# Score units one piece earlier in two steps, one query tile transposed by DMA, one bound from sums of squares

## The chip, the cores and the metric

The kernel runs on one core of a Trainium2 chip. The metric is the device time of one execution in microseconds (us); the median of several is quoted. The record calls an execution slow when it is over 1.5% above the fastest of its kernel, and fast otherwise; ratios use the fast ones.

In the profiles PE is TensorE (matmuls), PEld its weight loads, DVE VectorE, ACT ScalarE, POOL GpSimd; SPq is the queue of SyncE, which here issues the stores and the transposes by DMA. L435 is line 435 of the kernel; the change shifts the lines, so the same instruction is L439 after it.

## The reference, cut to what matters

```python
scores = scale * np.matmul(q, k.transpose(0, 1, 3, 2))      # 8 batches, 8 heads, 576 tokens, head_dim 64
...
scores = np.where(causal, -1000000000.0, scores + np.minimum(bias, 0.0))
scores = scores - np.max(scores, axis=-1, keepdims=True)
attn = np.exp(scores)
attn = attn / (np.sum(attn, axis=-1, keepdims=True) + 1e-09)
x = np.matmul(attn, v)        # then as x: 4608 tokens x 512
...
h = x @ w_in                  # 512 -> 2048, layer 1
g = 0.5 * h * (1.0 + erf(h * inv_sqrt2))
out = g @ w_out               # 2048 -> 512, layer 2
```

The output is 4608 x 512 in fp32.

## The kernel before: the parts that matter

The MLP (layers 1 and 2) runs over nine chunks of 512 tokens. While chunk c is in it, the attention of batch b = c + 1 is threaded through chunk c's layer 2. This layer 2 has four sub-tiles of 128 tokens, 16 matmuls each, in 16 pieces of 4 matmuls; after each piece come the side items listed for it.

```python
def groups(c, subs, side):
    n = len(side)
    for i in range(n):
        l2_item(c, subs, i * FT // n, (i + 1) * FT // n)   # matmuls; at the end of a sub-tile copy and store
        for f, *a in side[i]:
            f(*a)

# chunks 1 to 6 (b = c + 1)
sc_at = (2, 5, 7, 9) if b < 4 else (2, 5, 8, 11)           # score units: 16 or 24 matmuls, then two exps on ACT
...
for at, (g, u) in zip((5, 8, 10 if b < 4 else 11, 12 if b < 4 else 14), ...):
    side[at].append((mk, b, g, u))                         # causal mask, DVE
for at, (g, it) in zip((6, 7, 9, 10), [(0, 0), (0, 1), (1, 0), (1, 1)]):
    side[at].append((av, b, g, it))                        # P @ V on PE, reciprocal and x on DVE
if b < 4:
    side[12].append((av, b, 0, 2))
    side[13].append((av, b, 1, 2, True))                   # True: no transpose by DMA
    side[14].append((to_xT, b, 2, True))                   # four PE transposes and a DVE copy
if c == 1:
    side[0].extend([(absmax, c, 0), (absmax, c, 1)])
    side[3].append((cert_exp,))
```

An x tile must be transposed into xT before layer 1 reads it: by PE, or by a DMA from SP's queue:

```python
def to_xT(b, it, pe=False):
    ...
    if not pe:
        nc.sync.dma_start_transpose(out=xT[:, :, t0 : t0 + n], in_=x[:n, :])
        return
    ...
```

A certificate at the end checks that bounds on q, k and v hold, among them the largest |q| and |k|. It takes them from absmax (a reduction on DVE) or, for batch 0, from sums of squares (ACT, accumulated). Otherwise a slow general path runs; it never does on this data.

## Time and profile before

| | before |
|---|---|
| median, first three executions | 315.59 us |
| span of the profiled run, granted clock | 314.2 us, 0.999 |
| PE / DVE / ACT busy | 96% / 63% / 61% |
| layer 2 of chunk 1 | 70.77 to 89.02 us: 18.24 us |
| layer 2 of chunk 2 | 103.80 to 121.88 us: 18.08 us |

The lengths of phases are the differences between the starts of the first matmul of each layer in the timeline (o_ps is layer 2, h_ps layer 1), taken before rounding. The two phases, as the answer on windows gives them for the kernel before; columns are length, then busy time and number of instructions of PE, weight load, DVE, ACT, POOL, the clock, the share of DMA and GB/s:

```profile
70.77:89.02 18.25, 17.90 (x187) 8.97 (x189) 15.04 (x25) 11.90 (x12) 2.60 (x4) 1.00 0.76 171
...
103.80:121.88 18.08, 17.82 (x186) 9.14 (x188) 12.74 (x36) 11.34 (x11) 2.60 (x4) 1.00 0.79 174
```

PE is full in both, DVE is not; yet step 1 is 0.16 us longer than step 2, and the list of waits has one entry that says why:

```profile
PEld L435 <- DVE P L367: 0.6, 1, 0.6
```

One P @ V product (P is the matrix of exps of the scores, masked) had its weight load held up for 0.6 us by a mask on DVE; it is the first product of step 1, at 78.42 us.

### The profile page before, as it was taken

What the parts mean: (1) busy time and instruction counts of PE and PEld (TensorE: products, weight loads), DVE (VectorE), ACT (ScalarE), POOL (GpSimd) and SP (SyncE); (2) the same over time, 40 slices, a digit from 0 to 9 for tenths busy, and PEclk for the clock granted to TensorE, in tenths of its full rate; (3) what the DMA queues carried; (4) which work ended last, traced back from release to release, by engine and by line L of the source; (5) the groups of instructions that cost most, each with busy time, mean ns of one, the idle gap of its engine ahead of it and who ended that gap; (6) DMA issues with size and microseconds to landing.
All of it is one profiled execution on the core that took longest, in us unless ns stands there. A gap on an engine that the chain in (4) does not pass through costs nothing. (4 is left out here: it accounts for less than half of the span.)

```text
span 314.2 us, 6059 instructions
## 1 busy us (share of the span) xinstructions
PE 302.0 (96%) x2475; PEld 155.5 (49%) x2516; DVE 199.0 (63%) x398; ACT 191.0 (61%) x258; POOL 54.5 (17%) x73
## 2 busy tenths in 40 slices
PE   8899999999999999999999999999999999999993
PEld 3477755544554455545454455444544555444441
DVE  7776658599769856975598459955895532250020
ACT  2786878887737673875586658756776666105400
POOL 8653341133001500070007000500000000000000
PEclk9999999999999999999999999999999999999999
DMA  7999999779521973179307951633101331010012
GB/s 124 222 230 209 225 211 270 163 140 211 141 84 25 199 173 102 22 166 206 102 17 171 190 118 36 143 79 91 50 19 42 102 52 26 33 72 32 1 68 75
DMA packets 30979, 36.46 MB, mean 116 GB/s; under 512 B 15648, under 2 KB 20000, under 8 KB 30944
## 3 DMA queue, kind: packets, MB, share of 16 engines
q0 software_dynamic: 11552, 23.07, 38.1%
q1 hardware_dynamic: 19248, 12.80, 14.4%
q8 instruction: 21, 0.34, 0.4%
q14 instruction: 14, 0.11, 0.1%
q10 hardware_dynamic: 144, 0.13, 0.1%
HBM read 36.85 MB, written 9.44 MB: 147 GB/s over the span
## 5 line engine op out<-in xcount | busy, mean ns | idle before, releaser
L483 PE MATMUL o_ps<-w_out_r,gT 128*128 128x512 bf16 x551 | 132.2, 379 | 2.4 <-issue 1.6
L467 PE MATMUL h_ps<-xT,w_in_r 128*128 128x512 bf16 (+1 forms) x625 | 131.4, 357 | 1.3 <-DVE xT L413 0.5
L472 ACT ACTIVATE gT<-h_ps 128x1024 bf16<-128x1024 f32 (+1 forms) x80 | 75.1, 939 | 64.5 <-PE h_ps L467 63.7
L467 PEld LDWEIGHTS <-w_in_r 128*128 128x128 bf16 x640 | 59.8, 98 | 54.2 <-issue 0.6
L483 PEld LDWEIGHTS <-gT 128*128 128x128 bf16 x576 | 51.9, 98 | 56.6 <-issue 3.0
L359 ACT ACTIVATE P<-sc_ps 128x1024 bf16<-128x1024 f32 x56 | 54.3, 1021 | 30.5 <-PE sc_ps L344 30.5
L122 POOL DMA_DIRECT2D raw_v<-in_v_dram x40 | 34.1, 863 | 128.4 <-ACT sq L213 115.7
L493 DVE COPY o_sb<-o_ps 128x512 f32<-128x512 f32 x31 | 21.4, 691 | 46.5 <-PE o_ps L483 46.5
L444 DVE RECIPROCAL rc<-av 128x4 f32<-128x4 f32 (+1 forms) x80 | 14.0, 175 | 39.4 <-PE av L435 39.3
L187 DVE STREAM_TRANSPOSE qkT<-raw_qk 128x576 f32<-128x576 f32 x32 | 37.4, 1242 | 1.8 <-DMA raw_qk<-in_k_dram 1.7
L445 DVE TENSOR_TENSOR x<-av,rc 128x256 bf16<-128x256 f32 (+1 forms) x80 | 33.8, 423 | 3.0
L435 PEld LDWEIGHTS <-P 128*128 128x128 bf16 x576 | 27.1, 97 | 16.5 <-issue 0.8
L205 DVE TENSOR_REDUCE amx<-raw_qk 128x2 f32<-128x2304 bf16 x14 | 35.1, 2532 | 0.0
L435 PE MATMUL av<-vv,P 128*128 128x65 bf16 x576 | 30.5, 193 | 0.6 <-POOL vv L221 0.2
L367 DVE TENSOR_TENSOR P<-P,tri_bf 128x1024 bf16<-128x1024 bf16 (+1 forms) x33 | 22.0, 669 | 9.1 <-ACT P L359 9.1
L221 DVE TENSOR_TENSOR vv<-raw_v,wb 128x512 bf16<-128x512 f32 (+1 forms) x39 | 25.4, 690 | 2.5 <-DMA raw_v<-in_v_dram 2.5
L213 ACT ACTIVATE sq<-raw_v 128x512 bf16<-128x512 f32 (+1 forms) x40 | 24.8, 621 | 0.0
L344 PE MATMUL sc_ps<-qkT 32*128 32x256 bf16 (+2 forms) x560 | 18.2, 250 | 0.0
L344 PEld LDWEIGHTS <-qkT 32*128 32x128 bf16 x560 | 11.7, 92 | 12.4 <-issue 11.6
L498 ACT ACT_TABLE_LOAD x8 | 10.3, 1283 | 0.9 <-PEq L817 0.8
L419 PE MATMUL f_ps<-zero 128*128 128x512 bf16 x26 | 9.3, 494 | 1.2 <-DVE zero L150 1.2
L501 ACT ACT_TABLE_LOAD x8 | 10.3, 1283 | 0.1
(81 smaller groups left out, 92.3 us busy)
## 6 DMA issues: line engine op xcount, KB each, us to landing
out_dram<-o_sb SPq DMA_DIRECT2D x35, 256.0 KB, 2.2
raw_v<-in_v_dram POOLq DMA_DIRECT2D x32, 256.0 KB, 5.5
raw_qk<-in_q_dram POOLq DMA_DIRECT2D x7, 576.0 KB, 7.5
raw_qk<-in_k_dram POOLq DMA_DIRECT2D x7, 576.0 KB, 10.4
w_in_r<-in_moe_w_in_dram POOLq DMA_DIRECT2D x4, 512.0 KB, 12.1
w_out_r<-in_moe_w_out_dram POOLq DMA_DIRECT2D x4, 512.0 KB, 15.8
raw_v<-in_v_dram POOLq DMA_DIRECT2D x8, 128.0 KB, 6.4
raw_qk<-in_q_dram POOLq DMA_DIRECT2D x2, 288.0 KB, 6.2
```

Of the source, the lines that this page charges most:

```text
L122: eng.dma_start(out=t[:n_st, st, :, :], in_=bass.AP(tensor=v.tensor, offset=v.offset + b * H * S * D + st * 128 * D, ap=[[D, n_st], [S * D ...
L187: nc.vector.transpose(qkT[b % 2][:, i, g, :S, :].rearrange("p s e -> p (s e)").bitcast(fp32) .rearrange("p (l j) -> p j l", j=LT), raws[b, ...
L205: nc.vector.tensor_reduce(amx[:, b * HG + g], raws[b, "qk"][:, :, g, :], axis=AX, op=ALU.max, apply_absolute_value=True,)
L213: nc.scalar.activation(sq[:n_st], raws[b, "v"][:n_st, st].rearrange("p h d -> p (h d)"), func=AF.Square, accum_out=sumv[:n_st, b, st : st ...
L221: eng.tensor_tensor(vv[b % 2][:n_st, st, :, 0:D], raws[b, "v"][:n_st, st, :, :], w.unsqueeze(2).to_broadcast([n_st, H, D]), op=MULT,)
L344: nc.tensor.matmul(s_ps[h // 2][:, h % 2, off : off + n], lhsT=qk[r, 1, g, jt * 128 : jt * 128 + 128, e], rhs=qk[r, 0, g, i0 : i0 + n, e], ...
L359: nc.scalar.activation(P[:, 2 * h2 : 2 * h2 + 2, o : o + 512], s_ps[h2], func=AF.Exp, scale=scale)
L435: nc.tensor.matmul(o_ps[:, h, :], lhsT=P[:, h, off : off + 128], rhs=vv[b % 2][:, jt, 4 * g + h, :], start=(i == 0), stop=(i == len(BLK[it ...
L445: nc.vector.tensor_tensor(x_of[b, it][:n, g * 256 : g * 256 + 256].rearrange("p (h d) -> p h d", d=D), o_ps[:n, :, 0:D], rc[:n].unsqueeze( ...
L467: nc.tensor.matmul(h_ps[:, i, :], lhsT=w_in_r[:, ko, ft * 128 : (ft + 1) * 128], rhs=xT[:, ko, c * NB + n0 : c * NB + n1], start=(ko == 0) ...
L472: nc.scalar.activation(gT_of[c][:, f2 * 2 : f2 * 2 + 2, n0:n1], h_ps, func=AF.Gelu)
L483: nc.tensor.matmul(y_of[c, sub], lhsT=gT[:, ft, sub * 128 : (sub + 1) * 128], rhs=w_out_r[:, ft, :], start=(ft == 0), stop=(ft == FT - 1),)
```

## The change

It has three parts, for steps 1 and 2 (chunks 1 and 2). The score units, the first mask and the products of query tiles 0 and 1 move up one piece of layer 2; the other three masks and the products of tile 2 move up two. Query tile 2 is transposed by DMA and no longer by PE. And the bound for batch 1's group 1 is taken by two squares on ACT, so that DVE has one absmax (2.5 us) less ahead of step 1's masks.

```diff
-                sc_at = (2, 5, 7, 9) if b < 4 else (2, 5, 8, 11)
+                sc_at = (1, 4, 6, 8) if b < 4 else (2, 5, 8, 11)
...
+                mk_at = (4, 6, 8, 10) if b < 4 else (5, 8, 11, 14)
...
+                av_at = (5, 6, 8, 9) if b < 4 else (6, 7, 9, 10)
...
                 if b < 4:
-                    side[12].append((av, b, 0, 2))
-                    side[13].append((av, b, 1, 2, True))
-                    side[14].append((to_xT, b, 2, True))
+                    side[10].append((av, b, 0, 2))
+                    side[11].append((av, b, 1, 2))
                 if c == 1:
-                    side[0].extend([(absmax, c, 0), (absmax, c, 1)])
+                    side[0].append((absmax, c, 0))
+                    side[12].extend([(square_qk, c, 1, 0), (square_qk, c, 1, 1)])
```

(Cut: `square_qk` gets the batch as an argument, and the certificate adds 0.25 to three pairs of sums in three small instructions.)

More of the change, by code (lines that the diff above doesn't have):

```diff
@@ L191, in tr_qk, with square_qk @@
         )
-    ssq = const.tile([128, HG, 2], fp32, name="ssq")
-    def square_qk(g, i):
-        r = raws[0, "qk"][:, i, g, :]
+    ssq = const.tile([128, 2 * HG, 2], fp32, name="ssq")
+    BY_SQ = [(0, 0), (0, 1), (1, 1)]
+    def square_qk(b, g, i):
+        r = raws[b, "qk"][:, i, g, :]
         nc.scalar.activation(
             r, r, func=AF.Square, scale=D ** -0.5,
-            accum_out=ssq[:, g, i : i + 1],
+            accum_out=ssq[:, b * HG + g, i : i + 1],
         )
@@ L288, in cert_1 @@
         cg[0] = g = const.tile([128, 3], fp32, name="cg")
-        nc.vector.tensor_scalar(amx[:, 0:HG, :], ssq, 0.25, None, op0=ALU.add)
+        for bb, gg in BY_SQ:
+            j = bb * HG + gg
+            nc.vector.tensor_scalar(amx[:, j], ssq[:, j], 0.25, None, op0=ALU.add)
         for i in range(2):
@@ L628 @@
                 side[9] = [(av, b, 0, 3)]
-                side[11] = [(av, b, 1, 2, True), (scale_v, b, 4), (square_qk, 0, 0), (square_qk, 0, 1)]
-                side[12] = [(av, b, 1, 3, True), (square_qk, 1, 0), (square_qk, 1, 1)]
+                side[11] = [(av, b, 1, 2, True), (scale_v, b, 4), (square_qk, 0, 0, 0), (square_qk, 0, 0, 1)]
+                side[12] = [(av, b, 1, 3, True), (square_qk, 0, 1, 0), (square_qk, 0, 1, 1)]
                 side[13] = [(to_xT, b, 2, True)]
@@ L642 @@
                 side[sc_at[3]].append((gelu_set,))
-                for at, (g, u) in zip((5, 8, 10 if b < 4 else 11, 12 if b < 4 else 14), [(0, 0), (1, 0), (0, 1), (1, 1)]):
+                mk_at = (4, 6, 8, 10) if b < 4 else (5, 8, 11, 14)
+                for at, (g, u) in zip(mk_at, [(0, 0), (1, 0), (0, 1), (1, 1)]):
                     side[at].append((mk, b, g, u))
-                for at, (g, it) in zip((6, 7, 9, 10), [(0, 0), (0, 1), (1, 0), (1, 1)]):
+                av_at = (5, 6, 8, 9) if b < 4 else (6, 7, 9, 10)
+                for at, (g, it) in zip(av_at, [(0, 0), (0, 1), (1, 0), (1, 1)]):
                     side[at].append((av, b, g, it))
                 if b < 4:
-                    side[12].append((av, b, 0, 2))
-                    side[13].append((av, b, 1, 2, True))
-                    side[14].append((to_xT, b, 2, True))
+                    side[10].append((av, b, 0, 2))
+                    side[11].append((av, b, 1, 2))
                 if c == 1:
-                    side[0].extend([(absmax, c, 0), (absmax, c, 1)])
+                    side[0].append((absmax, c, 0))
+                    side[12].extend([(square_qk, c, 1, 0), (square_qk, c, 1, 1)])
                     side[3].append((cert_exp,))
```

## The prediction

> **What bounds the kernel now.** I read the page first (engine shares, then the groups), then the timeline of all engines through layer 2 of chunk 2, then the answer on the tile xT, then the waits. The page, with PE's clock row and the groups that the change touches:
>
> ```profile
> PE 302.0 (96%) x2475; PEld 155.5 (49%) x2516; DVE 199.0 (63%) x398; ACT 191.0 (61%) x258; POOL 54.5 (17%) x73
> ...
> PEclk9999999999999999999999999999999999999999
> ...
> L205 DVE TENSOR_REDUCE amx<-raw_qk 128x2 f32<-128x2304 bf16 x14 | 35.1, 2532 | 0.0
> ...
> xT<-x SPq DMA_TRANSPOSE x29, 2.4
> ```
>
> PE is busy 96% of a 314.2 us span at full clock; DVE and ACT have slack on average. So the time is the length of PE's instruction stream plus its few gaps. Time saved on DVE or ACT counts only where PE waits for it. The change touches the layer-2 phases of chunks 1 and 2 only (steps 1 and 2; batches 2 and 3 are then in attention). The end of step 2 before, from the timeline of all engines:
>
> ```profile
> 115.04 0.64 PE L344 MATMUL sc_ps<-qkT 32*128 32x256 bf16 x24
> 115.61 0.30 PE L435 MATMUL av<-vv,P 128*128 128x65 bf16 x4
> 115.72 1.94 ACT L359 ACTIVATE P<-sc_ps 128x1024 bf16<-128x1024 f32 x2 [0.72 <-PE sc_ps L344]
> ...
> 117.31 0.17 DVE L444 RECIPROCAL rc<-av 128x4 f32<-128x4 f32 x1
> 117.52 0.42 DVE L445 TENSOR_TENSOR x<-av,rc 128x256 bf16<-128x256 f32 x1
> 117.67 1.28 ACT L501 ACT_TABLE_LOAD   x1
> 117.92 0.69 DVE L493 COPY o_sb<-o_ps 128x512 f32<-128x512 f32 x1
> ...
> 118.53 0.68 DVE L367 TENSOR_TENSOR P<-P,tri_bf 128x1024 bf16<-128x1024 bf16 x1
> ...
> 119.33 0.18 DVE L444 RECIPROCAL rc<-av 128x4 f32<-128x4 f32 x1
> ...
> 120.80 0.39 PE L410 MATMUL xt_ps<-ident_bf,x 128*128 128x128 bf16 x4
> ...
> 121.88 0.59 PE L467 MATMUL h_ps<-xT,w_in_r 128*128 128x512 bf16 x2
> ```
>
> Columns are start, duration, engine, line, operation. PE goes from the last score unit (115.04) through the PE transposes (120.80) to the next chunk's layer 1 (121.88) with no hole over 0.1 us. In step 1 the same marks are 82.16, 87.93 and 89.02. The transposes by DMA, from the answer on xT:
>
> ```profile
> L406 SPq DMA_TRANSPOSE xT<-x x29: 1171/1196/1992, 62.0 to 264.1; - x29
> ...
> DMA to landing us min/median/max: 2.3/2.4/7.0
> ```
>
> A DMA transpose takes SP's queue 1.2 us and lands 2.4 us after issue as a median, worse when the loads are running.
>
> **What the Trainium skill says.** (1) "TensorE: Matmul & The Clock Gate", Part 4: PE-mode transpose: the result goes to PSUM and needs a DVE copy after; about 390 ns alone, 275 ns in one kernel. Here the four transposes of a tile are pipelined: PE's next matmul starts 0.22 us after the first of them (120.80 to 121.02), and the copy is the 0.42 us row at 121.22. (2) "VectorE: DVE Perf Modes", The three transpose paths: 1309 ns for a 128x128 block by DMA; the trace has 2.4 us for four blocks with their completion, and that is what I use. (3) The same page, The perf-mode tier table: tensor_reduce runs at 1x only. The trace agrees: 2532 ns for 2304 elements, the costliest single DVE instruction. (4) "DMA: Bandwidth & Descriptors", Issuing engines are not separate DMA queues: all DMAs share the same 16 engines. The trace agrees: the two transposes issued at 181.2 and 182.5 us, when loads still run (the table of windows gives a DMA share of 1.09 at 178 to 180 and 0.73 at 180 to 182 us), land after 4.1 and 3.2 us instead of 2.4.
>
> **The change, part by part.**
> Which token tiles matter: layer 1 of chunk c reads tokens 512c to 512c+511. For chunk 2 that includes batch 2 (from token 1152) up to its token 384, so query tiles 0 to 2; for chunk 3 it is batch 3's tiles 0, 1 and half of 2. Tile 2 must therefore be in xT before the first matmul of the next layer 1. That is why it was transposed on PE, close to its use.
>
> (a) PE transposes removed: four in each of two steps, 0.22 us of PE stream each step, on the path: -0.44 us. The copy (0.42 us of DVE) also goes; it is off the path.
>
> (b) All score units, masks and attention-times-V products go up one piece of layer 2 (4 matmuls; eight take 116.86 to 118.58, so 0.86 us a piece). Nothing is added on PE, order and spacing remain. The first unit now comes 8 matmuls after the start of layer 2, 72.5 us in step 1; it needs the PSUM tile of the last gelu, free at 71.99. No new wait.
>
> (c) One absmax (2.5 us) leaves DVE in step 1. Before, the four ran 67.25 to 77.16, so the first mask came at 77.69 to 78.36 and PE's first product at 78.42: the waits list 0.6 us of PEld behind that mask in one case. The distance from second score unit to end of the fourth is 76.72 to 82.75 = 6.03 us in step 1 against 109.75 to 115.61 = 5.86 us in step 2, where DVE is not late. So it is worth 0.17 us.
>
> (d) Two ACT squares with their accumulator reads, about 1.15 us each by the four that exist (52.78 to 57.37 is 4.59). They come after the gelu table load ending at 86.1; ACT then sat idle 4.92 us before the gelu at 91.00. Hidden. The two extra small DVE operations in the certificate, in the last chunk, are some 0.3 us by neighbours of 0.14 to 0.2, off the path.
>
> (e) Added: a DMA transpose of tile 2 whose landing PE must await. The chain from the end of the last score unit, with before's own durations: to the exp's start 0.11 (115.61 to 115.72), two exps 1.94, hand-over 0.03, mask pair 0.80 (118.53 to 119.33), reciprocal and x of group 0 0.61 (117.31 to 117.92), the store's copy 0.61 (117.92 to 118.53; the instruction order puts it between the two x), reciprocal and x of group 1 0.63, SP's start 0.06, landing 2.45, PE's restart 0.05 (estimate, from other hand-overs). Sum 7.29 us. PE's own work in the same stretch: before 121.88 - 115.61 = 6.27, less 0.22 transposes, plus one piece 0.86 = 6.91. **So PE arrives 0.38 us early and waits.**
>
> The end of the step: the last score unit ends at 115.61 - 0.86 = 114.75 in step 2, and at 82.75 - 0.86 - 0.17 = 81.72 in step 1. Adding 7.29: layer 1 starts at 122.04 (before 121.88: +0.16) and 89.01 (before 89.02: -0.01). **Sum +0.15 us.** I add 0.05 for the 256 KB store of the third sub-tile, which SP issues just ahead of the transpose on the same rings: 315.59 + 0.2 = 315.8.
>
> **The rivals.**
> 1. The transpose is hidden. Then the gain is what PE loses: 0.22 in step 2, 0.39 in step 1, so 315.0. For it: DMA is quiet there (the share of DMA is 0.09 at 116 to 118 us). Against it: the chain above, short by 0.38 us in both steps.
> 2. The transpose lands late, as under load (3.2 to 4.1 us): PE waits 0.8 to 1.7 us more in each step, 317 to 319. For it: the store just ahead in the queue. Against it: that store's own landing is 2.2 us after issue, in both steps, and the big loads of step 2 end near 116 us, of step 1 near 82 us.
> 3. DVE was a hidden bound in step 1, so that freeing 2.5 us shortens it by more. Against: DVE idles 1.31 us before the reciprocal at 83.09, so it has caught up by then; I count 0.17.
> 4. ACT becomes late for the next gelu: needs over 4.9 us of new work, there is 2.7 at most.
>
> **Range and chances.** The sum is +0.2; rival 1 gives -0.6, a partly late landing +1. I give the main chain about 60%, rival 1 25%, rival 2 10%. Runs of before lie within 0.4 us. The range is 315.0 to 316.6. 2% is 6.3 us, which no rival reaches: within 2% at 0.97, faster 0.01, slower 0.02.
>
> **What would show each step.** In the changed profile: L410 group down from 44 to 36 transposes and 31 DMA transposes instead of 29; 13 absmax, 6 squares of raw_qk; the first mask of step 1 no longer holding up PE; a wait of PE (or PEld) at L1's first matmul (layer 1) for a DMA xT of 0.3 to 0.5 us, twice, which does not exist before; layer 1 of chunks 2 and 3 starting within 0.3 us of 89.0 and 121.9. The prediction is wrong if that wait is absent, or is over 1 us because the landing of these two transposes is over 3 us, or if later phases, which I take as a mere shift, change length.

## The result and the profile after

The changed kernel took 315.64 us (median of 6 runs, 314.98 to 316.12), the kernel before 315.7 us in the same rounds (6 runs, 314.78 to 316.66). The ratio is 0.9994, 95% interval 0.997 to 1.0017: the same. The ratio is made from the fast runs of the same rounds, so not quite the ratio of the medians.

From the page of the changed kernel, the lines of PE and of the absmax group:

```profile
PE 305.0 (97%) x2508; PEld 155.0 (49%) x2508; DVE 196.2 (62%) x397; ACT 193.4 (62%) x262; POOL 54.5 (17%) x73
...
L207 DVE TENSOR_REDUCE amx<-raw_qk 128x2 f32<-128x2304 bf16 x13 | 32.6, 2535 | 0.0
```

One absmax is gone (2.5 us less on DVE). PE's busy time seems to rise by 3 us, but that is records and not work: the trace of before lacks 25 of the 576 layer-2 matmuls and 15 of the 640 of layer 1, this one lacks none. For the same reason no conclusion is drawn from PE's counts of these two groups. The counts that the prediction named came out: 36 PE transposes (44 before), 31 DMA transposes (29), 13 absmax, 6 squares; and the list of waits no longer has a product held up by a mask.

The end of step 2 in the changed kernel, from the timeline of all engines, the counterpart of the lines in the prediction:

```profile
114.01 0.64 PE L348 MATMUL sc_ps<-qkT 32*128 32x256 bf16 x24
...
114.58 0.30 PE L439 MATMUL av<-vv,P 128*128 128x65 bf16 x4
...
114.69 1.94 ACT L363 ACTIVATE P<-sc_ps 128x1024 bf16<-128x1024 f32 x2 [0.72 <-PE sc_ps L348]
...
116.66 0.69 DVE L371 TENSOR_TENSOR P<-P,tri_bf 128x1024 bf16<-128x1024 bf16 x1
...
117.47 0.17 DVE L448 RECIPROCAL rc<-av 128x4 f32<-128x4 f32 x1
...
118.02 0.68 DVE L497 COPY o_sb<-o_ps 128x512 f32<-128x512 f32 x1
118.03 3.62 PE L487 MATMUL o_ps<-w_out_r,gT 128*128 128x512 bf16 x16
...
118.73 0.34 SPq L499 DMA_DIRECT2D out_dram<-o_sb  x1
118.82 0.42 DVE L449 TENSOR_TENSOR x<-av,rc 128x256 bf16<-128x256 f32 x1
119.28 1.20 SPq L410 DMA_TRANSPOSE xT<-x  x1
...
121.82 1.89 PE L471 MATMUL h_ps<-xT,w_in_r 128*128 128x512 bf16 x8 [0.17 <-issue]
```

PE now does its last four pieces in one run, the 16 matmuls from 118.03. Matmuls of this size start every 0.216 us, so the next could start at 121.49. It starts at 121.82: a hole of 0.33 us, of which the row shows 0.17 (the end of the row before is modelled). The label "issue" says that the profile found no releaser. The transpose was issued at 119.28; its landing, asked for that instruction alone:

```profile
L410 SPq DMA_TRANSPOSE xT<-x x1: 1195/1195/1195, 119.3 to 119.3; - x1
...
DMA to landing us min/median/max: 2.5/2.5/2.5
```

Taken before rounding, the transposes of tile 2 landed at 88.76 and 121.73 us, and layer 1 began 0.09 us after them in both steps. So the time fits the DMA, but the profile doesn't name it; this needed experiments.

Phase by phase, from these two traces:

| phase | before | changed |
|---|---|---|
| layer 1 of chunk 1 | 14.30 | 14.30 |
| layer 2 of chunk 1 (step 1) | 18.24 | 18.18 |
| layer 1 of chunk 2 | 14.78 | 14.78 |
| layer 2 of chunk 2 (step 2) | 18.08 | 18.20 |
| each phase of chunks 3 to 7 and layer 1 of chunk 8 | the same in both | within 0.01 |
| from layer 2 of chunk 8 to the end | 19.18 | 19.32 |

Before rounding, step 1 is 0.06 us shorter and step 2 is 0.11 us longer. All else is a shift, except the very end. That end and the stretch ahead of chunk 1 differ between any two runs: in the ten traces the former is 18.50 to 19.90 us, and the start of chunk 1's layer 2 lies between 69.68 and 71.60 us. They differ between runs of the same kernel too (70.67 and 71.60 us in the two traces of the changed kernel), so they count here as noise of the total time.

### The profile page after: what moved, and what is told of

It reads as the page before. It is cut to its first block, busy times and chain, and to the rows that moved or that the text cites. A ratio compares the mean times of both kernels' runs of the same rounds, so it can differ in the third digit from the quotient of the medians.

```text
span 314.3 us, 6094 instructions
## 1 busy us (share of the span) xinstructions
PE 305.0 (97%) x2508; PEld 155.0 (49%) x2508; DVE 196.2 (62%) x397; ACT 193.4 (62%) x262; POOL 54.5 (17%) x73
## 5 line engine op out<-in xcount | busy, mean ns | idle before, releaser
L487 PE MATMUL o_ps<-w_out_r,gT 128*128 128x512 bf16 x576 | 135.6, 379 | 0.0
L207 DVE TENSOR_REDUCE amx<-raw_qk 128x2 f32<-128x2304 bf16 x13 | 32.6, 2535 | 0.0
```

Source lines behind the costliest of these rows:

```text
L207: nc.vector.tensor_reduce(amx[:, b * HG + g], raws[b, "qk"][:, :, g, :], axis=AX, op=ALU.max, apply_absolute_value=True,)
L487: nc.tensor.matmul(y_of[c, sub], lhsT=gT[:, ft, sub * 128 : (sub + 1) * 128], rhs=w_out_r[:, ft, :], start=(ft == 0), stop=(ft == FT - 1),)
```

## The experiments

The theory: taking the transposes off PE and the mask wait out of step 1 saves about 0.6 us, but PE then waits 0.33 us for the DMA transpose of tile 2, in both steps, and that gives it back. The rival: the hole ahead of layer 1 is a start-up cost that the profile calls issue and has nothing to do with the DMA. Eight runs were made, of six new kernels and two repeats, all correct. The phases of the two steps:

| run | step 1 | step 2 | ratio to before of its rounds |
|---|---|---|---|
| before | 18.24 | 18.08 | |
| changed | 18.18 | 18.20 | 0.9994 (0.997 to 1.0017) |
| changed, again (e7) | 18.16 | 18.18 | 0.9984 (0.997 to 0.9997) |
| e1: tile 2 on PE again | 18.09 | 18.09 | one run |
| e2: store emitted later | 17.86 | 17.86 | 0.9988 (0.995 to 1.0025) |
| e8: e2 again | 17.86 | 17.86 | 0.9957 (0.9943 to 0.9971) |
| e3: an extra DMA transpose | 19.58 | 19.54 | 1.007 (1.0043 to 1.0097) |
| e4: before, tile 2 by DMA only | 19.68 | 19.52 | 1.0074 (1.0051 to 1.0096) |
| e5: absmax back on DVE | 19.18 | 18.16 | 1.0007 (0.9988 to 1.0026) |
| e6: before, squares only | 18.09 | 18.09 | one run |

**e1, the transposes of tile 2 on PE again.**

```diff
-                    side[11].append((av, b, 1, 2))
+                    side[11].append((av, b, 1, 2, True))
+                    side[14].append((to_xT, b, 2, True))
```

> The changed kernel, but query tile 2 is transposed on PE again (four transposes and the DVE copy, three pieces after its last product); everything else of the change stays. Theory (the new transpose by DMA lands 0.33 us after PE has run dry, and this wait eats what the change saves): the hole ahead of layer 1 in chunks 2 and 3 is gone, 0.22 us of transposes are back, so both layer-2 phases take 18.08 us instead of 18.18 and 18.20; span 0.2 us shorter than the changed kernel. Rival (the hole is a start-up cost of layer 1 that the profile calls issue, and has nothing to do with the DMA): the hole stays at 0.16 us or more and both phases take 18.4 us.

Measured: 18.09 us in both. With the transposes back on PE the steps are 0.1 us shorter than with the DMA. So in the place where it stands, the DMA transpose costs more PE time (0.33 us of hole) than the 0.22 us it removes. The single run of 315.0 us proves nothing by itself; the phases do. They are also those of e6 below (18.09), which moves nothing: moving the units up by itself saves no time, it only makes room for the DMA.

**e2, the store of the third sub-tile after the last product of tile 2.**

```diff
         for i in range(n):
-            l2_item(c, subs, i * FT // n, (i + 1) * FT // n)
+            l2_item(c, subs, i * FT // n, (i + 1) * FT // n, store=not (c in (1, 2) and subs == (2,)))
...
                     side[11].append((av, b, 1, 2))
+                    side[11].append((l2_store, c, (2,)))   # the copy and store of l2_item, as a function
```

> The changed kernel, but in chunks 1 and 2 the copy and store of the third sub-tile are emitted after the last product of query tile 2, so that the reciprocal and x of group 1 no longer stand behind the 0.61 us copy on DVE, nor the transpose behind the store on the queue. Theory: the transpose is issued 0.6 us earlier, lands 6.7 us after the end of the last score unit, PE needs 6.9 us, so PE no longer waits: both phases take 17.86 us (0.33 us less than the changed kernel's), span 0.66 us shorter than the changed kernel, time ratio against before about 0.998. Rival (start-up cost): phases unchanged at 18.2 us, no gain.

Measured: 17.86 us in both phases, as the theory said. The end of step 1 in e2, from PE's own timeline:

```profile
84.09 3.62 PE L487 MATMUL o_ps<-w_out_r,gT 128*128 128x512 bf16 x16
87.55 1.89 PE L471 MATMUL h_ps<-xT,w_in_r 128*128 128x512 bf16 x8
```

From the first of the 16 matmuls to layer 1 it is 3.46 us, which is 16 times 0.216; in the changed kernel it was 3.78 and 3.79 us (85.07 to 88.85, 118.03 to 121.82). The hole is gone, and nothing was done to layer 1. A start-up cost would have stayed: the rival is out. The transpose of tile 2 in step 1:

```profile
L410 SPq DMA_TRANSPOSE xT<-x x1: 1190/1190/1190, 85.0 to 85.0; - x1
...
DMA to landing us min/median/max: 2.5/2.5/2.5
```

Before rounding it landed at 87.42, 0.13 us ahead of layer 1 at 87.55 (0.15 in step 2). In the runs in which PE waits, layer 1 began 0.09 us after the landing, so the spare is about 0.04 to 0.06 us (an estimate from these numbers). One size was not as expected: counted from the product after the last score unit, the transpose was issued 4.32 us later (80.64 to 84.96), in the changed kernel 4.69 (81.62 to 86.31). That is 0.37 us earlier and not 0.6, since DVE, freed of the copy, now waits for PE's last products of tile 2 (83.85 to 84.26) before its reciprocal at 84.29. It was just enough.

**e3, one more DMA transpose ahead of tile 2's.**

```diff
+                    side[11].append((to_xT, b, 1))         # repeats tile 1, the same values
                     side[11].append((av, b, 1, 2))
```

> The changed kernel with one more DMA transpose on the same queue, a repeat of query tile 1 just ahead of that of tile 2, in steps 1 and 2; the result stays right. Theory: tile 2's transpose starts about 1.3 us later, PE waits that much longer, phases of 19.5 us each, 2.6 us in all. Rival (PE doesn't wait for this transpose): no change.

Measured: 19.58 and 19.54 us. The two transposes of step 1 on the queue, and the end of step 1 from PE's timeline:

```profile
85.89 2.50 SPq L410 DMA_TRANSPOSE xT<-x  x2
...
84.53 3.62 PE L487 MATMUL o_ps<-w_out_r,gT 128*128 128x512 bf16 x16
89.70 1.89 PE L471 MATMUL h_ps<-xT,w_in_r 128*128 128x512 bf16 x8 [1.56 <-issue]
```

The delay passes one for one to PE, again under the label "issue": 5.17 us between the two starts where 3.46 are matmuls. In this trace that label ahead of layer 1 is the wait for a landing. e2 moved the store along with the copy; e3 leaves both where they were, so it is the transpose that PE waits for and not the store. The kept traces say it more sharply: in the two steps of all five runs in which PE waits (changed, e7, e3, e4, e5) layer 1 began 0.09 us after the landing of tile 2's transpose, ten times of ten, whether the wait was 0.3 or 1.7 us. One run (granted clock 0.979) took 323.32 us.

**e4, tile 2 by DMA without moving the units.**

```diff
-                    side[13].append((av, b, 1, 2, True))
-                    side[14].append((to_xT, b, 2, True))
+                    side[13].append((av, b, 1, 2))
```

(This is an edit of the kernel before.)

> The kernel before with one thing changed: query tile 2 of batches 2 and 3 is transposed by DMA; no unit is moved, absmax stays. Theory: x of tile 2 is done 5.16 us after the end of the last score unit, the transpose lands 2.5 us later, so layer 1 starts 7.7 us after it instead of 6.27: each phase 1.43 us longer (19.67 and 19.51 us), 2.9 us in all, time ratio against before 1.009. Rival (taking transposes off PE is what counts): 0.44 us shorter.

Measured: 19.68 and 19.52 us, within 0.01 us of what the chain gave. The transposes by DMA alone make the kernel 0.7% slower; moving the units and tile 2's products up is what pays for their latency.

**e5, the absmax back on DVE, in the changed kernel.**

```diff
-                    side[0].append((absmax, c, 0))
-                    side[12].extend([(square_qk, c, 1, 0), (square_qk, c, 1, 1)])
+                    side[0].extend([(absmax, c, 0), (absmax, c, 1)])
```

(And the certificate's list of squares without (1, 1).)

> The changed kernel with the bound of batch 1's group 1 on DVE again (absmax, four in a row) and its two squares gone from ACT; units stay one piece up. Theory: the four absmax end at about 77.1 us on the clock of the kernel before (phase start plus 6.3 us); the copy of the first sub-tile (0.6) and the first mask (0.67) follow, so the mask is ready about 7.6 us after the start of layer 2 of chunk 1, while PE wants it after 6.5 us. PE stalls about 1.1 us in step 1, which passes on to the last score unit and the transpose: phase of chunk 1 is 19.2 us instead of 18.18; chunk 2 stays 18.2. Total +1.0 us against the changed kernel. Rival (DVE is off the path at 62% busy, the moved bound is worth 0.17 us at most): phase of chunk 1 is 18.2 to 18.35 us.

Measured: 19.18 us in step 1 and 18.16 us in step 2. From the timeline of all engines, step 1 of e5:

```profile
76.89 0.68 DVE L497 COPY o_sb<-o_ps 128x512 f32<-128x512 f32 x1
77.48 0.68 DVE L371 TENSOR_TENSOR P<-P,tri_bf 128x1024 bf16<-128x1024 bf16 x1
...
78.22 0.18 PEld L439 LDWEIGHTS <-P 128*128 128x128 bf16 x4 [1.45 <-DVE P L371]
78.22 0.30 PE L439 MATMUL av<-vv,P 128*128 128x65 bf16 x4 [0.96 <-DVE P L371]
```

DVE comes out of its reductions at 76.89 and does the copy and the mask, and PE waits 0.96 us for that mask. So the moved bound is no side matter: with the units one piece earlier it is worth 1.0 us (19.18 against 18.18), because the mask is wanted 0.86 us sooner than before.

**e6, the squares alone, in the kernel before.**

```diff
-                    side[0].extend([(absmax, c, 0), (absmax, c, 1)])
+                    side[0].append((absmax, c, 0))
+                    side[12].extend([(square_qk, c, 1, 0), (square_qk, c, 1, 1)])
```

(With the functions of the change; every position and the PE transposes stay as before.)

> The kernel before with only the bound of batch 1's group 1 taken from squares on ACT; no unit moved, tile 2 on PE. Theory: step 1 loses the wait for its first mask, 0.17 us, and so becomes like step 2: phases of 18.07 and 18.08 us (before: 18.24 and 18.08). Rival (the two squares make ACT late for the next gelu, or take the pair of exps back): a phase or the layer 1 after it (14.78 us) grows.

Measured: 18.09 and 18.09 us; layer 1 of chunk 2 stays at 14.78. Step 1 loses 0.15 us and becomes like step 2; ACT makes nothing late. The one time, 316.64 us, is above those of before although both steps are shorter: this run's end took 19.90 us, the longest of all.

**e7 and e8, the changed kernel and e2 once more, five rounds each on one chip.**

> The changed kernel once more, unchanged, for the spread of its phases and beside the next run. Both theories: phases of 18.2 us in chunks 1 and 2 again; time ratio against before 1.000 within 0.002. The stretch ahead of chunk 1's layer 2 and the stretch after chunk 8's layer 1 may differ by up to a microsecond, as they did between the earlier runs.

> The kernel with the store of the third sub-tile after tile 2's last product once more, for its time: the first five rounds had an outlier of 318 us and left the interval at 0.995 to 1.0025. Theory: phases of 17.86 us, 0.66 us below the changed kernel and 0.6 below before, so a ratio of 0.998 against before. If the ratio is 1.000 or over, the 0.6 us are given back elsewhere and the phases must show where.

Measured: the phases repeat to 0.02 us. In time the changed kernel is at 0.9984 (median 315.15 us of 6 runs, one of them 317.09), e2 at 0.9957 (median 314.3 us of 5 runs), before at 315.73 us. The interval of e2's second measurement excludes 1, that of the first (with a run of 318.03 us) does not. The phases account for 0.60 us, 0.19% of 315.7; the second ratio's interval is 0.29 to 0.57%. The rest isn't explained: in the traces of e2 and e8 the end of the kernel took 18.50 and 18.84 us, against 19.18 and more in before and the changed kernel, and the stretch ahead of chunk 1's layer 2 was 0.4 to 1.9 us shorter than in those; but e3, e4 and e5 had ends of 19.01, 18.81 and 18.82 too, and e1 a start of 69.90, so it may be chance. That remains open. Nor can the intervals be taken at their word here: that of e7 excludes 1 as well, though its two phases are 0.02 us longer than before's. Against the changed kernel of the same rounds e2 is at 0.9957/0.9984 = 0.997, where the phases (0.62 us) say 0.998. The execution of 318.03 us had a granted clock of 0.982, the lowest of its kernel. e2 is the fastest kernel, by 0.2% from the phases.

## Why the prediction was right

**The total.** Predicted 315.8 us and "same"; measured 315.64. But the forecast was 0.2 us above before, and the medians differ by -0.06 us (315.64 against 315.7): both are far inside the spread of single executions, so that the total came this close is partly luck. The forecast difference in the two phases was +0.15 us, measured +0.05 (and +0.02 in e7): at this size the agreement of the total says little, that of the parts says more.

**(a) The PE transposes, 0.22 us a step.** Held: e1 against e2 is 0.23 us (18.09 against 17.86), two kernels in neither of which PE waits for the DMA.

**(b) The units one piece up, without a new wait.** The prediction says that all masks and products go up one piece; three masks and tile 2's products go up two. Its chain nevertheless has the order of the new lists. The rest held: the product after the last score unit starts 10.95 us into the phase in both steps (81.62 less 70.67, 114.58 less 103.63), which is what the forecast had. It needed (c), however.

**(c) The absmax, 0.17 us.** Against the kernel before it held: 0.15 us in e6. But the prediction treated it as a part that stands alone. e5 shows that without it the change costs step 1 0.94 us against before (19.18 against 18.24): the same part is worth 1.0 us once the mask is wanted a piece earlier. The gain of a part was read from the old placement of the others.

**(d) The squares hidden on ACT.** Held: layer 1 after step 1 is unchanged in e6 and in the changed kernel.

**(e) The chain of 7.29 us to the landing of tile 2.** Measured 7.23 and 7.24 us (81.62 to 88.85, 114.58 to 121.82). The hole was 0.33 us, predicted 0.38. Two terms were off and partly cancel: the reciprocal and x of group 0 took 0.55 us (117.47 to 118.02), not 0.61, and PE began 0.09 us after the landing, not 0.05. The extra 0.05 us for the store ahead on the queue was not needed: the landing was 2.45 and 2.46 us, and 2.45 and 2.43 in e2 without it. e2 and e3 move the issue by -0.37 and +1.4 us, e4 to another place, and PE follows each time where the chain is the longer.

**The rivals.** The hidden transpose (rival 1) was wrong for the changed kernel, and right for e2. The late landing (rival 2) did not come. DVE as a larger bound (rival 3) was not seen against before: the part is 0.15 us there (e6), as the prediction counted; with the units moved it is one, see (c). ACT late (rival 4) did not come.

**What the prediction had wrong in form.** It said that the profile would show PE or PEld waiting 0.3 to 0.5 us for a DMA xT. The profile shows two waits labelled "issue", 0.16 and 0.17 us on PE's rows (0.63 and 0.64 on PEld's), PE's being half the hole, since the end of the matmuls ahead is modelled and no releaser was inferred. By its own sign ("wrong if that wait is absent") a reader of the label alone would have called it wrong; the landing times and e2 and e3 show that the wait is there.

## What to carry to other kernels

Work moved off the bound engine only pays if its result is back before that engine runs dry: add up the latency chain from the last event that both share, and compare it with the bound engine's work left from the same event. Where the chain is a little too long, look in it for work that only stands there by order of emission: here a store's copy (0.6 us) and its DMA, moved behind the urgent transpose, brought it forward by 0.37 us and turned an even trade into a gain of 0.4 us in one step and 0.2 in the other. And when a consumer is moved earlier, the slack of every producer shrinks with it.

## What the Trainium skill lacked or had wrong

- "VectorE: DVE Perf Modes", The three transpose paths, gives 1309 ns for 128x128 by DMA and doesn't say from what to what. Here a DMA transpose of four such blocks within SBUF took the queue 1.2 us and landed 2.4 to 2.5 us after issue, also with a 256 KB store issued 0.55 us ahead of it on the same queue. No page of the skill gives the time from issue to landing for it on this chip.
- "TensorE: Matmul & The Clock Gate", Part 4: PE-mode transpose, gives 390 ns alone and 275 ns in a kernel. Four in a row cost PE's stream 0.22 us together (e1 less e2: 0.23 us), so 0.055 us each; the single latency does not tell what they cost when PE is the bound.
- No page of the skill says how a matmul's wait for a DMA landing looks in the profile: here it is a hole labelled issue, 0.17 us for 0.33 in the changed kernel and 1.56 us for 1.71 (5.17 less 3.46) in e3.
